# Stage 1 of a fused attention and gated-MLP kernel: one visit of the column halves for the early queries instead of two

## The chip, the cores and the metric

The kernel runs on one core of a Trainium2 chip. The metric is the device time of one execution in microseconds. The time before is 681.13 us, the median of three runs (680.72 to 682.45). The granted TensorE clock of the profiled execution is 0.999 of full speed over the whole span.

## The reference, cut to what matters

The program computes three stages one after another: plain attention with rotary positions, a gated MLP with spatial mixing, and a top-2 mixture of four causal attention experts. The change lies in the first stage alone:

```python
scores = scale * np.matmul(q_rot, k_rot.transpose(0, 1, 3, 2))   # 4 x 8 heads, 576 x 576, head_dim 64
scores = scores - np.max(scores, axis=-1, keepdims=True)
attn = np.exp(scores)
attn = attn / (np.sum(attn, axis=-1, keepdims=True) + 1e-09)
return np.matmul(attn, v)
```

## The kernel before, in words

Stage 1 works on 16 groups, each a pair of heads of one batch entry (`Work`, group number n). In a group the 576 queries of two heads make nine score blocks x = 0 to 8 of 128 rows: x = 2i + j is query block i of head j, and block 8 holds the last 64 queries of both heads. `slot(k)` (line 526) writes one step of the pipeline; k = 9n + x, and there are 9 slots in a group. The text calls them slot 0 to slot 8, and T5 is the start of the first score product that slot 5 issues. Lines 634 and 47 to 61 fix the order on TensorE (PE), ScalarE (ACT), VectorE (DVE) and GpSimd (POOL) to the order in which the code is written (`keep_in_program_order`). Most DMAs on SyncE's queue (SP) are not in that fixed order; the framework places them.

In slot x the code issues, in this order:

- on ACT the exponentials of block x (`exps`, line 449), which read the block's scores in PSUM (tile ps_S, two buffers) and write tile e (four buffers); in slots 0 and 4 also a copy of the finished products of the group before (`out`);
- on PE the scores of block x+1 (`scores`, line 434: four products of 288 columns, six for block 8), then the four transposes of block x-1 (`turn`, line 454, into ps_t, two buffers), then in slots 4, 5, 7, 0 and 1 one transpose of the 64 leftover keys (`turn_left`, into ps_l);
- on DVE the row maxima of block x+1 (`maxima`, tile nmax), and in odd slots a small gather of leftovers;
- the copy of the transposed block x-1 from PSUM to g0 or g1 (`place`, line 459): ACT for head 0 (even blocks), DVE for head 1 (odd blocks);
- on PE the products with the values (`av`, line 487). Queries 256 to 575 are done in slots 1 and 3 of the next group. Queries 0 to 255 of the group need the placed blocks 0 to 3 (g0) and are done in three parts: key blocks 0 and 1 in slot 5, key blocks 2 and 3 in slot 7, the leftover keys in slot 8. In the first two parts the weights are 64 columns wide: head 0 writes partitions 0 to 63 and head 1 partitions 64 to 127 of tile ps_o, so each head uses its own half of the array's columns (64-column records, `128*64` in the trace). The text calls such a run of 64-column products a visit. The leftover part is one product of full width;
- the preparation of the groups n+1 and n+2: rotary products on POOL (`rope`, slots 4 and 7), splits into high and low parts on DVE and POOL (`parts`, slots 1 and 3), whose DMAs fill the key operand kh (`fill_k`) that the scores of the next group's block 0 read in slot 8, and loads (slots 3 and 4).

After each slot the main loop (lines 648 to 666) advances side work: conversion of a weight for stage 2 (`convert_in`, some slots of all groups; its DVE steps use the same PSUM tile ps_l as `turn_left`), and from group 4 on, once per group, one step of `attended(bx, 0)` (line 268), which prepares stage 2's input: a load step (one DMA sa<-xr, three DMAs sr<-rd; groups 4, 6, 8, 13), a norm step (a POOL product and a DMA; groups 5, 7, 9, 14) or a part step (an ACT cast and a POOL subtraction; groups 10, 11, 12, 15).

Of the kernel before, what the change touches and what calls it, by code (L numbers as in the profile page):

```python
# [44 lines left out]
def fused_kernel(ctx, tc, qk, v, w_in, w_out, w_sg, g_ln, b_sg, wqk, wvg, wo, rope, cst, out):  # L45
# [222 lines left out]
    def attended(pool, b):  # L268


        ts = {}

        def load(c):
            ts[c] = a, r = [pool.tile([P, S], F32, tag="s" + x, name="s" + x, bufs=k) for x, k in (("a", 3), ("r", 2))]
            nc.sync.dma_start(a, xraw[b][c])
            factor_in(r, rd[b][c])

        def norm(c):
            a, r = ts[c]
            POOL.tensor_tensor(a, a, r, op=ALU.mult)  # L280
            nc.sync.dma_start(xd[b][c], a)

        def part(c):
            if c == 0 and b == 1:
                t = wc.tile([P, 2, 4, S], F32R, tag="w", name="x")
                xs[b] = [t[:, 0], t[:, 1]]
            elif c == 0:
                xs[b] = [pool.tile([P, 4, S], F32R, tag="x" + x, name="x" + x) for x in "hl"]
            split(*[x[:, c] for x in xs[b]], ts[c][0])

        order = (((load, 0), (norm, 0), (load, 1), (norm, 1), (load, 2), (norm, 2), (part, 0), (part, 1),
                  (part, 2), (load, 3), (norm, 3), (part, 3)) if b != 1 else
                 ((load, 0), (norm, 0), (load, 1), (norm, 1), (part, 0), (load, 2), (norm, 2), (part, 1),
                  (load, 3), (norm, 3), (part, 2), (part, 3)))
        for do, c in order:
            do(c)
            yield
# [3 lines left out]
    def leftover(pool, b):  # L301

        a, r = [pool.tile([P, S], F32, tag="s" + x, name="e" + x, bufs=k)[:, 0:512]
                .rearrange("p (c i n) -> p c i n", c=4, i=2) for x, k in (("a", 3), ("r", 2))]
        for i in range(2):
            nc.sync.dma_start(a[:, :, i, :], xraw[b + i][:, :, 512:S].rearrange("c p n -> p c n"))
            for j in range(2):
                h = slice(64 * j, 64 * j + 64)
                d = rd[b + i][:, 4, h].rearrange("(o c) n -> o c n", o=1)
                nc.sync.dma_start(r[h, :, i, :], d.to_broadcast([64, 4, 64]))  # L310
        yield
        POOL.tensor_tensor(a, a, r, op=ALU.mult)
        yield
        xe[b] = [pool.tile([P, 4, P], F32R, tag="e" + x, name="e" + x) for x in "hl"]
        split(*[x.rearrange("p c (i n) -> p c i n", i=2) for x in xe[b]], a)
        yield
# [7 lines left out]
    with ExitStack() as st:  # L324
# [7 lines left out]
        wk = st.enter_context(tc.tile_pool(name="a_wk", bufs=2))  # L332
# [193 lines left out]
        def slot(k):  # L526


            n, x = divmod(k, 9)
            (nk, xk), (nn, xn) = divmod(k - 1, 9), divmod(k + 1, 9)  # L530
            w, p, wk, wn, nx = [works.get(i) for i in (n, n - 1, nk, nn, n + 1)]

            if w:
                w.exps(x)
            if x == 0 and p:
                p.out(False)
            if x == 4 and p:
                p.out(True)

            if wn:  # L540
                if xn == 0:
                    wn.start()
                wn.scores(xn)
            if wk:
                wk.turn(xk)
            for at, g, i in ((4, w, 0), (5, w, 1), (7, w, 2), (0, p, 3), (1, p, 4)):
                if x == at and g:
                    g.turn_left(i)
            if x == 1 and p:
                p.turn_factor()  # L550

            if wn:
                wn.maxima(xn)
            for at, g, i in ((1, w, 0), (3, w, 1), (5, w, 2), (7, w, 3), (0, p, 4)):
                if x == at and g:
                    g.gather(i)
            if x == 0 and p:
                p.factor(0)

            if n == 0 and x in (2, 3):  # L560
                works[1].rope(3 - x, (2,), DVE)
            if wk:
                wk.place(xk)
            if x == 0 and p:
                p.factor(1)
            if x == 2 and p:
                p.place_left(True)
                p.store_factor()
            if x == 5 and w:
                w.place_left(False)  # L570

            if x in (1, 3) and p:
                p.av(True, x // 2)
            if x in (5, 7, 8) and w:
                w.av(False, {5: 0, 7: 1, 8: 2}[x])

            if nx:
                if x == (4 if n == 0 else 1):
                    nx.parts(0, DVE if n else ACT)
                if x == 3:  # L580
                    nx.parts(1, DVE if n else ACT)
                if n + 2 < B * NP:
                    if x == 3:
                        works[n + 2] = Work()
                        works[n + 2].load(n + 2)
                    if x == (7 if n == 0 else 4):
                        works[n + 2].rope(0)
                    if x == (8 if n == 0 else 7):
                        works[n + 2].rope(1)
                if x == 4 and n + 2 < B * NP:  # L590
                    works[n + 2].load_values()
# [37 lines left out]
        def warmed(n):  # L629

            for _ in range(n):
                PE.matmul(warm[:, 0:P], zero, zero, start=True, stop=True)
# [15 lines left out]
        for k in range(9 * B * NP + 7):  # L648
            n, x = divmod(k, 9)
            slot(k)  # L650
            if k < 4:
                warmed(2)
            if x in W_AT[4 if n == NP * B - 1 else min(n, 2 + n % 2)]:
                next(wload, None)
            if k == 9 * 4:
                steps = attended(bx, 0)
            if k == 9 * 14:
                lsteps = leftover(bx, 0)
            if n >= 4 and x == 8:
                next(steps, None)  # L660
            if n >= 14 and x == 3:
                next(lsteps, None)
            if k == 9 * 15 + 1:
                nsteps = attended(bx, 1)
            if k > 9 * 15 and x in (1, 5):
                next(nsteps, None)
# [37 lines left out]
    with ExitStack() as st:  # L704
        def pool(name, bufs):
            return st.enter_context(tc.tile_pool(name=name, bufs=bufs, reuse_waits="tile"))

        psum(st, t=1, c=1, S=3)
        wst, sm, ge, wp, wk, bg = (pool("b_st", 1), pool("b_sm", 2), pool("b_ge", 1), pool("b_w", 1),
                                   pool("b_wk", 2), pool("b_big", 1))  # L710
# [204 lines left out]
        for b in range(1, B):  # L915
# [7 lines left out]
            if b == 2:  # L923
                w = wc.tile([P, 12, DM], F32R, tag="w", name="w")
# [28 lines left out]
    with ExitStack() as st:  # L953
# [4 lines left out]
        sm, wk, bg, ptp = (pool("c_sm", 2), pool("c_wk", 2), pool("c_bg", 1), pool("c_pt", 1))  # L958
# [462 lines left out]
        w, g = works[2 * B - 1], op[B - 1]  # L1421
# [103 lines left out]
```

## Time and profile before

| what | value |
|---|---|
| median of three runs | 681.13 us |
| the profiled execution's own time | 678.8 us |
| its span, first to last instruction | 677.0 us |
| PE busy | 666.6 us (98%) |
| DVE, ACT, POOL busy | 454.1, 426.2, 342.6 us |
| granted TensorE clock | 0.999 |
| stage 1 | from about 13 to 271 us of the span |

Times are from one profiled execution. A row of the timeline gives the start of a run of like instructions in us from the start of the span, how long the run lasted to the end of its last instruction, the engine, the line (here that of a helper, so the tile names tell the instructions apart: ps_S are scores, ps_t and ps_l transposes, ps_o products with values, g placed blocks, e exponentials), the shape, the number of instructions, and in brackets the idle time before it with what ended it. PE's instructions are pipelined: the end of a run overlaps the start of the next, so the cost of a run is read from start to start. A float32 product makes two records. PEld is the weight load of TensorE.

### The profile page before, as it was taken

To read this page: it belongs to the slowest core of one execution; us is meant where nothing else is said; L and a number is where in the kernel's file an instruction comes from. 1 tells how busy PE (TensorE), PEld (TensorE's weight loads), DVE (VectorE), ACT (ScalarE), POOL (GpSimd) and SP (SyncE) were. 2 spreads that over 40 slices of the span, in tenths; PEclk is the share of its full clock that TensorE was granted. 3 is DMA by queue.
4 is the path that set the end of the run, shared out by engine and by line. 5 is a ranking of instruction groups with operands and counts; after the bars stand their busy time and mean duration, and the time that the engine had idled before them with its cause. 6 is when DMAs were issued, how large, how long until landed. Compare 5 with 4: busy or idle time off the path is not lost.

```text
span 677.0 us, 13577 instructions
## 1 busy us (share of the span) xinstructions
PE 666.6 (98%) x4741; PEld 585.9 (87%) x4741; DVE 454.1 (67%) x1026; ACT 426.2 (63%) x1018; POOL 342.6 (51%) x333
## 2 busy tenths in 40 slices
PE   8999999999999999999999999999999999999997
PEld 8777777777777777798999899899999999999985
DVE  5877777777787767478974764665247667666674
ACT  6777676777777777574472472472147776666774
POOL 2877777788888861462446217306313451542320
PEclk9999999999999999999999999999999999999999
DMA  7698887888788762652365234045556364453522
GB/s 271 197 282 246 258 235 210 247 243 248 229 250 249 215 175 80 190 157 80 118 186 176 88 108 135 16 132 161 128 167 163 76 185 93 131 158 81 142 82 78
DMA packets 64930, 112.84 MB, mean 167 GB/s; under 512 B 19471, under 2 KB 24670, under 8 KB 64862
## 3 DMA queue, kind: packets, MB, share of 16 engines
q1 hardware_dynamic: 62126, 106.30, 54.3%
q10 hardware_dynamic: 2736, 5.68, 2.8%
q8 instruction: 38, 0.62, 0.4%
q14 instruction: 30, 0.25, 0.1%
HBM read 58.06 MB, written 18.98 MB: 114 GB/s over the span
## 4 chain that ended last, share of the span: by engine, by line
PE 85%; DVE 5%; DMA 4%; ACT 2%; issue 1%; POOL 1%; SPq 1%; ACTq 0%; POOLq 0%; DVEq 0%
PE ps_S L59 45%; PE ps_o L59 16%; PE ps_t L59 13%; PE ps_f L59 5%; PE ps_l L59 3%; PE ps_s L59 3%; DVE nmax L59 1%; DMA ws<-in_w_sg_dram 1%; DVE ga L59 1%; DMA kh<-hi 1%; DMA mask<-in_cst_dram 1%; DVE g L59 1%; ACT ga L59 1%; DMA xr<-xt 1%; ACT e L59 1%
## 5 line engine op out<-in xcount | busy, mean ns | idle before, releaser
L59 ACT ACTIVATE e<-ps_S,nmax 128x576 f32<-128x576 f32 x144 | 108.0, 750 | 68.0 <-DVE nmax L59 67.8
L59 DVE TENSOR_REDUCE nmax<-ps_S 128x1 f32<-128x576 f32 x144 | 108.6, 755 | 57.3 <-PE ps_S L59 55.0
L59 PE MATMUL ps_t<-ident,e 128*128 128x128 f32 x776 | 120.6, 273 | 0.0
L59 PEld LDWEIGHTS ps_t<-ident,e 128*128 128x128 f32 x776 | 94.9, 140 | 3.8 <-ACT wih L59 0.4
L59 PE MATMUL ps_S<-kh,q 128*128 128x288 f32 x352 | 86.3, 337 | 2.6 <-ACT e L59 1.6
L59 POOL TENSOR_TENSOR t<-t,rp 128x576 f32<-128x576 f32 x60 | 84.4, 1429 | 0.1
L59 PEld LDWEIGHTS ps_S<-kh,q 128*128 128x128 f32 x352 | 53.2, 189 | 31.0 <-issue 10.7
L59 PE MATMUL ps_o<-g,v 128*64 128x320 f32 (+1 forms) x512 | 76.6, 418 | 0.4 <-DVE g L59 0.4
L59 POOL TENSOR_TENSOR lo<-t,hi 128x576 fp32r<-128x576 f32 x30 | 43.3, 1444 | 49.1 <-DVE hi L59 47.8
L59 PE MATMUL ps_S<-lo,qz 128*128 128x288 f32 x304 | 65.1, 296 | 0.0
L59 PEld LDWEIGHTS ps_o<-g,v 128*64 128x64 f32 x512 | 31.3, 136 | 25.1 <-issue 9.5
L59 PE MATMUL ps_S<-yh,w 128*128 128x288 f32 x256 | 51.8, 304 | 0.0
L59 POOL TENSOR_TENSOR yl<-x,yh 128x640 fp32r<-128x640 f32 (+1 forms) x16 | 25.1, 1569 | 51.1 <-ACT yh L59 50.9
L59 ACT ACTIVATE e<-e,nmax 128x128 f32<-128x128 f32 (+4 forms) x72 | 42.3, 588 | 13.6 <-DVE nmax L59 13.6
L59 PEld LDWEIGHTS ps_S<-lo,qz 128*128 128x128 f32 x304 | 48.5, 188 | 0.0
L59 ACT COPY g<-ps_t 128x512 f32<-128x512 f32 x80 | 46.8, 585 | 1.4 <-PE ps_t L59 0.8
L59 DVE COPY g<-ps_t 128x512 f32<-128x512 f32 x64 | 43.5, 680 | 1.3 <-PE ps_t L59 1.3
L59 POOL TENSOR_TENSOR t<-t 128x576 f32<-128x576 f32 x28 | 39.8, 1421 | 2.2
L59 PEld LDWEIGHTS ps_S<-yh,w 128*128 128x128 f32 x256 | 38.7, 189 | 0.1
L59 ACT ACTIVATE ga<-ga 128x512 f32<-128x512 f32 (+1 forms) x34 | 22.3, 656 | 25.8 <-DVE ga L59 25.8
L59 DVE CUSTOM_DVE_ANT_0 e<-ps_s,mask 128x128 f32<-128x128 f32 (+3 forms) x64 | 31.0, 485 | 8.1 <-PE ps_s L59 6.3
L59 PE MATMUL ps_S<-wsh,vh 128*128 128x288 f32 x160 | 34.6, 297 | 0.8 <-DVE u L59 0.5
(286 smaller groups left out, 1734.8 us busy)
## 6 DMA issues: line engine op xcount, KB each, us to landing
t<-in_qk_dram SPq DMA_DIRECT2D x32, 576.0 KB, 4.4
kh<-hi SPq DMA_DIRECT2D x92, 144.0 KB, 2.7
q<-hi SPq DMA_DIRECT2D x38, 144.0 KB, 2.4
qz<-hi SPq DMA_DIRECT2D x38, 144.0 KB, 3.1
q<-lo SPq DMA_DIRECT2D x38, 144.0 KB, 2.7
v<-in_v_dram SPq DMA_DIRECT2D x16, 320.0 KB, 3.0
sa<-xr SPq DMA_DIRECT2D x16, 288.0 KB, 3.6
xd<-sa SPq DMA_DIRECT2D x16, 288.0 KB, 2.9
```

The costliest lines, as they stand in the source:

```text
L59: ins = op(*a, **k)
```

## The change

Three edits, all in stage 1. In groups 0 to 14 (`nx` exists) slot 5 no longer turns and places block 4; slot 6 does so just before block 5, behind the scores of block 7. In the same groups the second part of the products for queries 0 to 255 (key blocks 2 and 3) moves from slot 7 to slot 5, right behind the first part. In groups 4 to 15 the step of `attended` runs after slot 4 instead of after slot 8. Group 15 keeps its old order of turns and products.

```diff
--- before.py
+++ after.py
@@ -541,7 +541,10 @@
                 if xn == 0:
                     wn.start()
                 wn.scores(xn)
-            if wk:
+            late = nx and x == 6
+            if wk and not (nx and x == 5):
+                if late:
+                    wk.turn(4)
                 wk.turn(xk)
             for at, g, i in ((4, w, 0), (5, w, 1), (7, w, 2), (0, p, 3), (1, p, 4)):
                 if x == at and g:
@@ -559,7 +562,9 @@
 
             if n == 0 and x in (2, 3):
                 works[1].rope(3 - x, (2,), DVE)
-            if wk:
+            if wk and not (nx and x == 5):
+                if late:
+                    wk.place(4)
                 wk.place(xk)
             if x == 0 and p:
                 p.factor(1)
@@ -571,8 +576,9 @@
 
             if x in (1, 3) and p:
                 p.av(True, x // 2)
-            if x in (5, 7, 8) and w:
-                w.av(False, {5: 0, 7: 1, 8: 2}[x])
+            if w:
+                for part in {5: (0, 1) if nx else (0,), 7: () if nx else (1,), 8: (2,)}.get(x, ()):
+                    w.av(False, part)
 
             if nx:
                 if x == (4 if n == 0 else 1):
@@ -656,7 +662,7 @@
                 steps = attended(bx, 0)
             if k == 9 * 14:
                 lsteps = leftover(bx, 0)
-            if n >= 4 and x == 8:
+            if n >= 4 and x == 4:
                 next(steps, None)
             if n >= 14 and x == 3:
                 next(lsteps, None)
```

## Rows read from the trace of the kernel before

**Rows 1.** The page, part 1: busy time of each engine.

```profile
PE 666.6 (98%) x4741; PEld 585.9 (87%) x4741; DVE 454.1 (67%) x1026; ACT 426.2 (63%) x1018; POOL 342.6 (51%) x333
```

**Rows 2.** Busy time by stretch, groups 3 to 10 whole; last columns clock, DMA share, GB/s.

```profile
62.84:190.03 127.19, 127.19 (x946) 98.55 (x945) 95.75 (x197) 93.07 (x241) 98.12 (x71) 1.00 0.83 239
```

**Rows 3.** Timeline of PE, group 8, slots 5 to 8 and the next slot 0.

```profile
151.14 0.51 PE L59 MATMUL ps_S<-kh,q 128*128 128x288 f32 x2
...
151.75 0.60 PE L59 MATMUL ps_t<-ident,e 128*128 128x128 f32 x4
152.19 0.27 PE L59 MATMUL ps_l<-ident,e 128*128 128x128 f32 x1
152.39 1.08 PE L59 MATMUL ps_o<-g,v 128*64 128x256 f32 x8
153.41 0.53 PE L59 MATMUL ps_S<-kh,q 128*128 128x288 f32 x2
...
154.04 0.60 PE L59 MATMUL ps_t<-ident,e 128*128 128x128 f32 x4
154.39 0.76 PE L59 MATMUL ps_S<-kh,q 128*128 128x288 f32 x4
...
155.70 0.27 PE L59 MATMUL ps_l<-ident,e 128*128 128x128 f32 x1
...
156.92 0.53 PE L59 MATMUL ps_S<-kh,q 128*128 128x288 f32 x2
...
158.23 0.61 PE L59 MATMUL ps_S<-kh,q 128*128 128x288 f32 x2
...
159.38 0.27 PE L59 MATMUL ps_l<-ident,e 128*128 128x128 f32 x1
159.43 0.40 PE L59 MATMUL ps_S<-kh,q 128*128 128x288 f32 x1
```

**Rows 4.** Timeline of the weight loads, group 8, at the end of slot 5's visit.

```profile
153.40 0.30 PEld L59 LDWEIGHTS ps_S<-kh,q 128*128 128x128 f32 x2 [0.39 <-ACT tl L59]
```

**Rows 5.** Timeline of DVE, group 8: the placing of block 3.

```profile
151.55 0.68 DVE L59 COPY g<-ps_t 128x512 f32<-128x512 f32 x1
```

**Rows 6.** Timeline of PE and DVE, group 0, slot 5: its visit and the placing before it.

```profile
22.95 0.65 PE L59 MATMUL ps_o<-g,v 128*64 128x256 f32 x2
23.28 0.67 DVE L59 COPY g<-ps_t 128x512 f32<-128x512 f32 x1
...
24.01 1.08 PE L59 MATMUL ps_o<-g,v 128*64 128x256 f32 x6 [0.41 <-DVE g L59]
```

**Rows 7.** Timeline of PE: a single visit in group 9, a double one in stage 1's tail.

```profile
160.81 1.30 PE L59 MATMUL ps_o<-g,v 128*64 128x320 f32 x8
...
273.52 2.37 PE L59 MATMUL ps_o<-g,v 128*64 128x320 f32 x16
```

**Rows 8.** Timeline of ACT, group 8: block 6 placed, exponentials of block 8.

```profile
155.90 0.59 ACT L59 COPY g<-ps_t 128x512 f32<-128x512 f32 x1
156.38 0.75 ACT L59 ACTIVATE e<-ps_S,nmax 128x576 f32<-128x576 f32 x1
157.02 0.20 ACT L59 ACTIVATION_READ_ACCUMULATOR e<-ps_S,nmax 128x1 f32 x1
```

**Rows 9.** Timeline of PE: groups 1, 2 and 12, the waits around slots 7 and 8.

```profile
42.76 0.60 PE L59 MATMUL ps_t<-ident,e 128*128 128x128 f32 x4
43.57 0.30 PE L59 MATMUL ps_l<-ident,e 128*128 128x128 f32 x1 [0.20 <-DVE wt L59]
...
61.55 0.49 PE L59 MATMUL ps_S<-kh,q 128*128 128x288 f32 x2 [0.79 <-DMA kh<-hi]
...
221.14 0.50 PE L59 MATMUL ps_S<-kh,q 128*128 128x288 f32 x2 [0.26 <-DMA xr<-xt]
```

**Rows 10.** DMA issues: the page (KB, us to landing), then SP's timeline in group 8.

```profile
kh<-hi SPq DMA_DIRECT2D x92, 144.0 KB, 2.7
...
151.10 2.86 SPq L154 DMA_DIRECT2D kh<-hi  x4
...
158.04 0.63 SPq L179 DMA_DIRECT2D sr<-rd  x1
```

## The prediction

> **What bounds the kernel now.** I read the page's busy times first: PE is busy for 98% of the span, every other engine for 67% or less [rows 1]. [...] So in stage 1 PE's own order of work sets the end, and the question is what PE's chain of starts becomes. For that I read PE's timeline of group 8 from start to start [rows 3]. What to see there: slot 5 starts at 151.14 and the next group's slot 1 at 159.43, 8.29 us later; all that the change moves on PE lies between. Last come the rows of DVE and ACT that would release PE if PE came earlier [rows 5, 8], for a PE that shows no idle time now may hide waits that it meets just in time.
>
> **What the change removes.** A visit of the column halves now takes 1.02 us, from 152.39 to 153.41 [rows 3]. Doubling it is cheaper than two: 16 records of 320 columns take 2.37 us where 8 take 1.30 [rows 7], 1.07 for eight more, which by columns is 0.86 for 256. A visit less its entry of 0.20 (152.19 to 152.39) gives 0.82; I take 0.84. What a second visit costs beyond its products is seen at its end: the next weight load stands still for 0.39 us [rows 4]. Without any new wait, slots 5 to 8 would be: slot 5, the leftover transpose at 0.61 (151.14 to 151.75, where block 4's turn stood), the visit at 0.81, then 1.02 + 0.84, so slot 6 at 2.67; slot 6, 0.98 (153.41 to 154.39) plus four transposes, 0.44 (151.75 to 152.19), 1.42; slot 7 without its visit, 1.31 to the leftover transpose (154.39 to 155.70) and 0.05 to the next scores (159.38 to 159.43), 1.36; slot 8 unchanged, 1.31 (156.92 to 158.23). Sum 6.76 against 7.09 now: 0.33 saved per group.
>
> **First new wait: DVE's placing of block 3.** Head 1's products read block 3, which DVE places from 151.55 to 152.23 [rows 5], 1.09 after the start of slot 5. Today the visit starts at 1.25, behind block 4's transposes, so the wait is hidden by 0.16. With these transposes gone PE is ready at 0.81. What happens then stands in group 0: head 0's two records start at 22.95, the rest waits for DVE until 24.01, although PE has nothing else to do; DVE's copy ended at 23.95, so the release takes 0.06 [rows 6]. In-order, head 0's lead is no use, as head 1's products still have to run whole. So head 1 starts at 1.15, not 0.81, and slot 6 starts at 1.15 + 1.02 + 0.84 = 3.01, slot 7 at 4.43. DVE cannot be earlier: this placing stands behind the maxima of block 5, which wait for slot 4's scores, and nothing there is moved. The wait, 0.34, eats the whole saving.
>
> **Second new wait: ACT in slot 8.** The scores that slot 0 issues go into the PSUM buffer that block 8's exponentials free. In group 8 ACT places block 6 at 155.90 (1.51 after slot 7 starts, just behind the transposes), starts the exponentials at 156.38 and ends their accumulator read at 157.22 [rows 8], 2.83 after slot 7's start, 2.89 with the release. Now the visit covers this: slot 0 starts 3.84 after slot 7 does. Without it PE comes at 1.36 + 1.31 = 2.67. So slot 0 starts at 4.43 + 2.89 = 7.32 instead of 7.10, and after a wait its scores take 0.63 (153.41 to 154.04), its transposes 0.44 and 0.05: the next slot 1 at 8.44 against 8.29 today. **Each regular group gets 0.15 us longer.**
>
> **What costs nothing.** ACT's placing of block 4 moves to slot 6. It starts 1.27 after that slot's start (0.63 + 0.44 + 0.20), frees ACT 0.48 later (155.90 to 156.38), so block 7's exponentials end near 2.6; the scores that need their buffer come at 1.42 + 1.36 = 2.78. If that cover is gone, PE waits up to 0.5 there. Block 4's tile e is held one slot longer, until slot 7's leftover transpose (1.31 + 0.27), before the exponentials of block 8 at 1.99 write over it. The step of `attended` at slot 4 instead of slot 8: four part steps put an ACT cast behind slot 4's copy, where ACT now has slot 5's placing time to spare, and a POOL subtraction ahead of the slot 7 rope products instead of behind them, so POOL ends the same; four norm steps move a POOL product and one DMA likewise; four load steps move four DMA issues on SP, about 0.6 each [rows 10], behind the kh issues of slot 3. Nobody needs these results before later groups. Bounds for the three together: 0.3 gained or lost in each of the twelve groups at worst, as no row shows POOL's or SP's order after the change; I take nothing, since all of them have more than a slot of room.
>
> **Groups that differ.** Group 0's visit waits already [rows 6], so it pays the 0.84 and 0.44 in full and gets back 5.04 - 4.01 = 1.03 from slot 7 on: +0.25. Group 1's leftover transpose in slot 7 waits for the weight conversion on DVE (43.57, where 42.76 + 0.44 = 43.20 would do [rows 9]); slot 7 comes over a microsecond later after slot 5 in the new order, so most of these 0.37 go: -0.2. In groups 2 and 12 slot 8 waits for a transfer, 0.79 and 0.26 of shown idle time [rows 9]; slot 8 would start at 5.79 against 5.78 now, so the transfer still ends last: 0. Group 15 keeps its order. Sum: 11 x 0.15 + 0.25 - 0.2 = +1.7; rounding in twelve terms can make 0.15 into 0.11 or 0.19, and I put the sum at 1.6. The profiled execution took 678.8 us with a span of 677.0; the median shown is 681.13, 2.3 higher, and the difference is applied to the median: 682.7.
>
> **Rivals.**
> (1) The waits do not bind, and the saved visit is a gain. With the first wait gone, the second would still hold slot 0 at 2.67 + 1.42 + 2.89 = 6.98, slot 1 at 8.10: 0.19 saved, over some 13 groups 2.5 us, 678.6. With both gone, 0.33 x 13 = 4.3, 676.8. For it speaks that PE has no idle time now [rows 2]; against it group 0, which waits in just this place [rows 6]. [...] Chance 0.17.
> (2) Transfers. The load steps' four issues (sa, three sr) come to stand ahead of kh's four in groups 4, 6, 8 and 13. The last kh issue of group 8 ends at 153.96 and lands some 2.7 later, 156.66, and the scores that read it start at 156.92 [rows 3, 10]: 0.26 of room. SP's order isn't fixed by the code, and it decides as soon as two of the four go first: 4 x 0.6 - 0.26 = 2.1 per group, 8 in all, 691; with one or two ahead 683 to 686. Against it: the code issues them a slot behind kh. Chance 0.10.
> (3) The order on PE, ACT, DVE and POOL is written out, so that the change does nothing is excluded, except for SP.
>
> **How the numbers follow.** A measurement of this kernel can tell 0.3%, 2.04 us, from no change. The forecast has 0.70 (0.03 is left for what I don't see); by its rounding and the bounds of the side steps about a quarter of it lies beyond +2.04, the rest within. Slower: 0.18 + 0.10 = 0.28. Faster: rival 1 nearly whole, 0.16. Same: 0.56. The range takes the forecast with its bounds (681 to 685) and reaches into rival 1's nearer case: 678.2 to 685.2. The likeliest case alone: 681.3 to 684.
>
> **What would show it.** In the changed trace, slot 5's ps_o run should split as in rows 6, with two records first and an idle weight load released by DVE g of some 0.3 us in groups 1 to 14; slot 6 should start 3.0 after slot 5; the first scores of slot 0 should carry a wait for ACT e, 2.9 after slot 7; a regular group should take 16.05 us instead of 15.90; the number of 64-column visits should fall by 15. No wait of the first kind, or a period below 15.8, proves rival 1. New waits for kh in groups 4, 6, 8, 13 prove rival 2. I am wrong in size if slot 6 starts later than 3.1, which would mean that the longer visit costs more than its products.

## The result, and the profile after

The changed kernel takes 685.79 us, the median of seven runs (682.97 to 688.89), the kernel before beside it 681.01 (679.66 to 682.45): 1.0072 times as long, 95% interval 1.0045 to 1.0099. Measured again later, beside the first try at t behind kh below, it was 681.94 against 679.37, 1.0038 [1.0017, 1.0058]. It is slower both times; the forecast was no change (682.7, range 678.2 to 685.2).

The profiled execution took 687.6 us with a span of 685.8, 8.8 longer than before's. All 8.8 lie in stage 1: from its end on, both kernels need 410 to 411 us. The page's busy times of the changed kernel:

```profile
PE 670.0 (98%) x4741; PEld 594.9 (87%) x4741; DVE 456.6 (67%) x1026; ACT 428.2 (62%) x1018; POOL 341.9 (50%) x333
```

Busy time by stretch, groups 3 to 10 whole (last columns clock, DMA share, GB/s), in this execution:

```profile
64.02:198.87 134.85, 130.09 (x947) 104.24 (x945) 97.25 (x198) 94.29 (x241) 97.33 (x71) 0.99 0.79 225
```

and the same eight groups in the profiled execution of its second measurement:

```profile
62.87:191.32 128.45, 128.19 (x945) 102.45 (x944) 96.87 (x198) 94.44 (x241) 98.75 (x72) 1.00 0.84 236
```

In [rows 2] PE was busy for all of 127.19. The second execution adds 1.26, or 0.16 a group, with one wait for a transfer (0.26, in group 8); its undisturbed groups take 16.02, 0.12 more than before's 15.90 (127.19 / 8), a price paid in every group. The first adds 6.4 more, and 4.76 of its stretch is PE idle: a price that differs from execution to execution. They have different causes.

**The price of every group.** PE's timeline of group 11, from slot 5 to the next slot 1 (the answer to [rows 3]):

```profile
191.56 0.51 PE L59 MATMUL ps_S<-kh,q 128*128 128x288 f32 x2
...
192.17 0.27 PE L59 MATMUL ps_l<-ident,e 128*128 128x128 f32 x1
192.37 2.27 PE L59 MATMUL ps_o<-g,v 128*64 128x256 f32 x16
...
195.99 0.77 PE L59 MATMUL ps_S<-kh,q 128*128 128x288 f32 x4
...
197.33 0.51 PE L59 MATMUL ps_S<-kh,q 128*128 128x288 f32 x2
...
198.87 0.53 PE L59 MATMUL ps_S<-kh,q 128*128 128x288 f32 x2
...
199.96 0.51 PE L59 MATMUL ps_S<-kh,q 128*128 128x288 f32 x2
```

DVE's placing of block 3 in the same group (answer to [rows 5]), the weight loads behind the visit and at the start of the next slot 0 (answer to [rows 4]), and ACT's exponentials of block 8 (answer to [rows 8]):

```profile
191.97 0.68 DVE L59 COPY g<-ps_t 128x512 f32<-128x512 f32 x1
```

```profile
194.57 0.30 PEld L59 LDWEIGHTS ps_S<-kh,q 128*128 128x128 f32 x2 [0.38 <-ACT e L59]
...
198.87 0.30 PEld L59 LDWEIGHTS ps_S<-kh,q 128*128 128x128 f32 x2 [0.30 <-ACT e L59]
```

```profile
197.98 0.74 ACT L59 ACTIVATE e<-ps_S,nmax 128x576 f32<-128x576 f32 x1
198.61 0.20 ACT L59 ACTIVATION_READ_ACCUMULATOR e<-ps_S,nmax 128x1 f32 x1
```

Slot 6 starts 3.01 after slot 5 (194.57 - 191.56; forecast 3.01), slot 7 at 4.43 (4.43), slot 0 at 7.31 (7.32), slot 1 at 8.40 (8.44, and 8.29 before). DVE ends the placing at 192.65, and in the trace the first record of head 1 starts at 192.70, as the first new wait had it. Slot 0 starts 0.06 behind ACT's accumulator read (198.81), as the second had it.

**The price that varies.** What PE waited for in stage 1 of the first execution (us in total, times, longest):

```profile
PE ps_S L59 <- DMA kh<-hi: 4.8, 3, 2.5
PE ps_S L59 <- ACT e L59: 2.9, 3, 1.3
```

Before, the first row was 0.8, once. Of the three waits in the second row two are in group 0, where the kernel before has them too; the third, 1.31, is at slot 8 of group 4. The longest wait for kh is in group 8. First PE's scores of slot 8, then the clock by stretch around them, then SP's issues ahead of them:

```profile
163.88 0.58 PE L59 MATMUL ps_S<-kh,q 128*128 128x288 f32 x2 [2.54 <-DMA kh<-hi]
```

```profile
160.50:163.80 3.30, 0.83 (x8) 0.59 (x6) 1.11 (x3) 1.73 (x5) 3.30 (x3) 1.00 0.69 170
163.80:167.40 3.60, 3.52 (x14) 3.35 (x15) 1.45 (x2) 1.31 (x4) 1.79 (x2) 0.55 0.74 256
167.40:170.40 3.00, 3.00 (x24) 2.17 (x22) 2.13 (x6) 2.28 (x6) 0.00 (x0) 0.97 0.65 219
```

```profile
156.59 0.36 SPq L365 DMA_DIRECT2D t<-in_qk_dram  x1
157.05 3.40 SPq L154 DMA_DIRECT2D kh<-hi  x4
160.55 1.82 SPq L511 DMA_DIRECT2D xr<-xt  x3
```

PE stood still for 2.54 us, and for the next 3.6 the granted clock was 0.55 of full speed: slot 8 took 2.20 and slot 0 1.87, where they take 1.30 and 1.10 after a short wait, 1.7 more. SP's rows show a load of raw queries or keys, t<-in_qk, ahead of the four kh transfers. SP's order belongs to the compiled kernel; both profiled executions of the changed kernel have the same. One t load stands ahead of kh in groups 2, 4 and 12 of the kernel before, and in groups 2, 4, 6, 8 and 12 of the changed one. The trace of before had its two transfer waits in groups 2 and 12 [rows 9].

Behind group 0 the first execution waited 1.31, 1.31, 0.91 and 2.54 us at slot 8 of groups 2, 4, 6 and 8, all with t ahead of kh, and nowhere else for more than 0.2. Its 8.8 us are, from these rows, some 1.5 for PE's order (13 groups of 0.12), 5.1 for groups 6 and 8 (3.45 of waits and 1.7 at the lower clock), where only the changed kernel has t ahead, and 1.8 more waiting in groups 2 and 4, where the kernel before has it too. But the order alone doesn't decide: the second execution, with the same order, waited only the 0.26.

So the theory to test was: (A) a t load ahead of kh delays kh; the moved step of `attended` adds such groups; PE's new order adds the small fixed price. Its rival (B): kh is late for another reason, and the order of t and kh doesn't matter.

### The profile page after: what moved, and what is told of

Read it like the earlier page. It is cut to its first block, busy times and chain, and to the rows that moved or that the text cites. A ratio compares the mean times of both kernels' runs of the same rounds, so it can differ in the third digit from the quotient of the medians.

```text
span 685.8 us, 13567 instructions
## 1 busy us (share of the span) xinstructions
PE 670.0 (98%) x4741; PEld 594.9 (87%) x4741; DVE 456.6 (67%) x1026; ACT 428.2 (62%) x1018; POOL 341.9 (50%) x333
## 4 chain that ended last, share of the span: by engine, by line
PE 82%; DVE 5%; DMA 5%; ACT 2%; issue 2%; SPq 1%; POOL 1%; ACTq 0%; DVEq 0%; POOLq 0%
PE ps_S L59 44%; PE ps_o L59 16%; PE ps_t L59 12%; PE ps_f L59 4%; PE ps_l L59 3%; PE ps_s L59 3%; DMA kh<-hi 2%; DVE nmax L59 1%; SPq L154 1%; DMA mask<-in_cst_dram 1%; DMA ws<-in_w_sg_dram 1%; DVE ga L59 1%; ACT e L59 1%; DMA sr<-rd 0%; DVE g L59 0%
## 5 line engine op out<-in xcount | busy, mean ns | idle before, releaser
L59 PE MATMUL ps_t<-ident,e 128*128 128x128 f32 x776 | 118.8, 274 | 0.2
L59 PEld LDWEIGHTS ps_o<-g,v 128*64 128x64 f32 x512 | 40.2, 136 | 22.6 <-issue 7.3
L59 POOL TENSOR_TENSOR xl<-sa,xh 128x576 fp32r<-128x576 f32 x12 | 17.7, 1480 | 42.0 <-ACT xh L59 35.9
```

The lines of the kernel that those rows point to most:

```text
L59: ins = op(*a, **k)
```

## The experiments

**One edit at a time.** Beside the same kernel before (680.3, median of 29 runs) ran the changed kernel with the step back at slot 8, and the kernel before with the step at slot 4.

In the changed kernel:

```diff
-            if n >= 4 and x == 4:
+            if n >= 4 and x == 8:
```

In the kernel before:

```diff
-            if n >= 4 and x == 8:
+            if n >= 4 and x == 4:
```

> The two edits on TensorE alone; the step of attended goes back behind slot 8. Theory T (the transfers): the step at slot 4 lets the framework put the load t<-in_qk of SP's queue ahead of the four kh<-hi in groups 6 and 8, and PE waits for kh there; the edits on PE cost only the two waits, 0.14 a group. Then this kernel takes 682.0 to 683.0, a regular group 16.0 to 16.1, and no wait for kh in groups 4, 6 and 8 above 0.3. Rival P (the new order on PE by itself makes kh late): 684.5 to 686, waits for kh over 0.8 in groups 4, 6 and 8.

> The kernel before with the step of attended behind slot 4, nothing else. Theory T: waits for kh of 0.5 to 2.5 in groups 4, 6 or 8, which the kernel before does not have; 683 to 685. Rival P: 680.5 to 681.7, no new wait for kh.

PE's edits alone: 682.55 (679.56 to 685.29), 1.0020 [1.0001, 1.0039]; regular groups 16.02, and one wait for kh, 0.31, in group 2. That is as theory T had it. The step alone: 682.34 (679.53 to 686.59), 1.0024 [0.9998, 1.0050]; this lies between the two theories, and the interval reaches no change. Regular groups take 15.90 as before, but in its profiled execution, the slowest of twelve, slot 7 of groups 2, 6, 8 and 12 took 4.95, 2.92, 4.29 and 4.96 instead of 2.53. The rows name kh in groups 2 and 12 (2.35 and 2.33), another transfer in group 8 (1.70) and ACT in group 6 (0.33).

SP's order has t ahead of kh in groups 2 and 4 with PE's edits alone, and in groups 2, 4, 6, 8 and 12 with the step alone. So the moved step adds groups 6 and 8; the two longest waits here are in groups where the kernel before has t ahead too, and group 2 is done before the first moved step runs. Each half costs about 2 us by medians. But single times spread by 6 us, so the shares were still uncertain.

**The merged visit without moving block 4's transposes.** The kernel before with one edit; the step stays at slot 8.

```diff
-            if x in (5, 7, 8) and w:
-                w.av(False, {5: 0, 7: 1, 8: 2}[x])
+            if w:
+                for part in {5: (0, 1) if nx else (0,), 7: () if nx else (1,), 8: (2,)}.get(x, ()):
+                    w.av(False, part)
```

> Only the merging of the visit in slot 5; block 4 is turned in slot 5 before it, as in the kernel before, and the step stays behind slot 8. Theory of the two waits: head 1's products find block 3 placed, so the first wait is gone; the wait for ACT's exponentials of block 8 stays. Slot 5 3.10, slot 6 0.98, slots 7 and 8 together 2.9, a group 15.70, so 0.2 less than before; 678.0 to 679.0. Rival: slot 8 comes 0.35 earlier against the transfers of kh, which then bind in most groups; 680 to 682. Rival: the first wait was not DVE's placing but the longer visit itself; then slot 5 is 3.4 and the kernel 682.5 or more.

679.71 (677.17 to 682.45), 0.9987 [0.9965, 1.0009]. Regular groups take 15.78 us, 0.12 less than before (15.70 was expected, and 678.0 to 679.0 in all), where the changed kernel's take 0.12 more. So merging is a gain in every regular group, though the total isn't clear of noise; moving block 4's transposes out from in front of the visit turns it into a loss.

**All loads of a group held in the written order.**

```diff
-                    if n < 2:
-                        tc.keep_in_program_order(d)
+                    tc.keep_in_program_order(d)
```

(and the same for the kh transfers)

> The changed kernel with the four kh<-hi and the loads t<-in_qk of stage 1 held in program order on SP, so that kh goes first in every group. Theory T: the waits for kh in groups 2 to 8 go, 681.5 to 683.0. Rival P: 684.5 to 686, as the waits stay. A third possibility: SP stands behind kh's wait for its cast and t comes late for rope on GpSimd, 684 and more with waits for t.

740.8 us, 1.0879: here t is issued a group later than otherwise, the rotary products on POOL wait for it (5.1, 6.2 and 5.2 us in groups 3, 4 and 5), what stands behind them comes late, and groups take 16.4 to 23.3 us. It says nothing on A and B, only that t must be early too.

**A first try at t behind kh.** The t loads are issued a group earlier in the code, in slot 5, and held behind kh; three kernels, and the changed kernel again.

```diff
+                ahead_ = 2 if n == 0 and x == 3 else 3 if x == 5 else 0
+                if ahead_ and n + ahead_ < B * NP:
+                    works[n + ahead_] = Work()
+                    works[n + ahead_].load(n + ahead_)
                 if n + 2 < B * NP:
-                    if x == 3:
-                        works[n + 2] = Work()
-                        works[n + 2].load(n + 2)
```

> The changed kernel once more, on the same chip as the three below. From the two halves measured apart (1.0020 for the edits on TensorE, 1.0024 for the step): about 1.0045 times the kernel before if the two add up, 1.007 as in the first measurement if the step costs more on top of the edits on TensorE.

> The kernel before with the same change of the load; kh goes first in every group. Theory T: the waits of groups 2 and 12 (0.86 and 0.33 in the first profile) go, 0.997 to 0.999. Rival: no difference, as these waits come from something else.

> The changed kernel, with the load t<-in_qk issued in slot 5 for three groups ahead (where the framework hoists it to anyway) and kh and t held in program order: t now goes behind kh on SP in groups 2, 6, 8 and 12, only group 4 still has it ahead. Theory T: waits for kh stay in group 4 alone, 1.0015 to 1.003 times the kernel before, what the edits on TensorE cost alone, or less. Rival (the DMA engines are simply too full, whoever goes first): 1.004 or more, with waits for kh or t elsewhere.

> The merged visit behind block 4's transposes, with the load behind kh in every group. Theory T: 15.78 for every group from 2 to 14, 0.995 to 0.997 times the kernel before, the fastest of all. Rival: slot 8 now comes 0.1 to 0.2 earlier against kh and waits appear, 0.998 or more.

Beside a kernel before of 679.37: change again 681.94; before with t behind kh 683.62, 1.0044 [1.0027, 1.0060]; changed kernel so 687.78, 1.0097; merged visit alone so 682.50, 1.0035. All were slower, by my own edit: it also put the loads of group 2 behind kh in group 0, whose rotary products came late (group 0 waited for q, up to 4.4 us). In the changed kernel so edited PE also waited for kh, 0.94, 2.00 and 1.89 in groups 2, 3 and 4, though t stands ahead of it in group 4 alone: the rival's sign, and a first hint that t ahead of kh isn't the only way to a late kh. The useful part is that in the kernel before so edited groups 2 to 10 took 15.89 to 15.96 and the waits of groups 2 and 12 were gone.

**The same without that flaw.** Group 0 issues its loads in slots 2 and 8, which leaves its order as it was.

```diff
-                ahead_ = 2 if n == 0 and x == 3 else 3 if x == 5 else 0
+                ahead_ = 2 if n == 0 and x == 2 else 3 if x == (8 if n == 0 else 5) else 0
```

The decisive pair is this order in the kernel before, against the same with one of the two t loads written in slot 3 ahead of kh in groups 1 to 12.

> The kernel before, with the loads of raw queries and keys (t<-in_qk) held behind the four kh transfers on SP in every group; group 0 keeps the order of before, which the earlier attempt did not. Theory A (a t load ahead of kh on SP delays kh and makes slot 8's scores wait): no PE wait for kh in any group, groups 2 to 14 at 15.90 us, the waits of groups 2 and 12 gone (0.86 and 0.33 in the trace of before), so 1 us less: ratio 0.998 to 1.000. Theory B (kh is late for other reasons, the order of t and kh does not matter): waits for kh remain in some groups, ratio 1.000 within 0.002.

> The same kernel as the one with t behind kh, with one difference: in groups 1 to 12 one of the two t loads (64 x 1152 elements twice, 576 KB) stands ahead of kh on SP. Theory A: waits of PE for kh at slot 8's scores in most of these twelve groups, 0.3 to 2 us each (2.4 in the worst groups seen so far), and where one is over 2 us a fall of the granted clock behind it: 5 to 15 us slower, ratio 1.007 to 1.022. Theory B: the same time as with t behind kh, within 0.2%, and no more waits than before has.

With t behind: 678.42 (677.81 to 680.73), 0.9972 [0.9956, 0.9988]. With t ahead: 685.69 (682.90 to 688.92), 1.0073 [1.0049, 1.0096]. The order of one load and kh is worth 7.3 us in twelve groups; A holds, B falls. A had waits in most of the twelve groups; the profiled execution with t ahead, the slowest of its eight, has them in six. PE's waits behind group 0, with t ahead (with t behind no row names kh):

```profile
PE ps_S L59 <- DMA kh<-hi: 7.2, 6, 2.2
```

SP's timeline in group 3, t ahead of kh, then PE's at the scores of slot 8 that read kh:

```profile
73.17 0.36 SPq L368 DMA_DIRECT2D t<-in_qk_dram  x1
73.63 2.41 SPq L154 DMA_DIRECT2D kh<-hi  x4
```

```profile
79.16 0.50 PE L59 MATMUL ps_S<-kh,q 128*128 128x288 f32 x2 [1.85 <-DMA kh<-hi]
```

The same two with t behind kh:

```profile
73.25 2.38 SPq L154 DMA_DIRECT2D kh<-hi  x4
...
78.23 0.91 SPq L367 DMA_DIRECT2D t<-in_qk_dram  x2
```

```profile
77.04 0.53 PE L59 MATMUL ps_S<-kh,q 128*128 128x288 f32 x2
```

The page's row of DMA issues (KB each, median us from issue to landing), with t behind, then with t ahead:

```profile
kh<-hi SPq DMA_DIRECT2D x92, 144.0 KB, 2.6
```

```profile
kh<-hi SPq DMA_DIRECT2D x92, 144.0 KB, 3.9
```

SP issues kh only 0.4 later (73.63 against 73.25), and with t behind, PE needs kh 1.41 after the last issue (75.63 to 77.04). With t ahead PE goes on 3.12 after it (76.04 to 79.16). So most of the delay isn't SP's time but the transfer's: kh's transfers of 144 KB each take 3.9 us to landing with t's 576 KB ahead of them and 2.6 with t behind. By what mechanism t holds kh up isn't shown, and whether t on another queue would spare kh wasn't tried.

**What is left in the changed kernel.** It and the merged visit with the same order of loads:

> The changed kernel with t behind kh on SP (all groups but group 4, where one t stays ahead). Theory A: no waits for kh except perhaps in group 4, regular groups 16.02 us, so what is left of the loss is the 0.12 to 0.15 per group of PE's own order: 1.5 to 2 us against before, ratio 1.002 to 1.003. Theory B: waits for kh in groups 2 to 8 as in the changed kernel, ratio 1.004 to 1.007.

> Only the merged visit (behind block 4's transposes, which stay where they were; the step of attended stays at slot 8), with t behind kh on SP. Theory A: regular groups 15.78 us as in the run of the merged visit alone, no waits for kh: 1.5 us less for the visit and 1 us less for the transfers, 676 to 678, ratio 0.995 to 0.998. Theory B: as the merged visit alone, 0.9987 within 0.002.

The merged visit: 677.42 (676.70 to 678.39), 0.9955 [0.9937, 0.9973], the best kernel of the study, ahead of both, though its profiled execution still has one wait for kh, 0.94 in group 3, where A had none. The changed kernel: 683.59 (679.47 to 688.29), 1.0039 [1.0014, 1.0064], more than A's 1.002 to 1.003 and widely spread, so t ahead of kh isn't all that its transfers suffer from. Its profiled execution, the shortest (679.47), shows what else there is. What SP's queue waited for in groups 4 to 9:

```profile
SPq L171 <- DMA t<-in_qk_dram: 6.3, 3, 2.8
```

L171 issues q: SP stood still until a t load had landed, and kh stands behind q. In that stretch the same kernel with the step at slot 8 and PE's old order has 1.9, twice. The longest of the three is in group 8:

```profile
146.54 0.73 SPq L171 DMA_DIRECT2D q<-hi  x1
150.16 0.46 SPq L171 DMA_DIRECT2D q<-lo  x1
```

POOL made the low part of this q from 145.32 to 146.74, so the rotary products didn't hold this q; SP's wait for t did, and t is a load for a later group. What the step changes in SP's order is that in groups 5, 7 and 9 its xd stands just ahead of t, and in groups 5 and 7 its three sr stand between t and q; with the step at slot 8 xd stands behind q, and the sr between t and q in groups 6 and 8. That t lands late because of this is argued from the order and not shown. Two kernels part PE's order from the step, both with t behind kh; a third takes away the first new wait by DVE's order alone.

```diff
+            early = wk and x == 4 and nx
+            if early:
+                wk.place(3)
             if wn:
                 wn.maxima(xn)
-            if wk and not (nx and x == 5):
+            if wk and not early and not (nx and x == 5):
```

> The changed kernel's work on PE (merged visit, block 4's transposes behind the next scores), but the step of attended back at slot 8, and t behind kh on SP in every group. Theory A (with the transfers out of the way only PE's own order is left, and that costs 0.12 per group): groups 2 to 14 at 16.02 us, no waits for kh, 1.3 to 1.8 us above the kernel before with the same order of loads (678.42 in the last comparison), so 679.7 to 680.3, single times within some 3 us of each other, ratio to before 0.998 to 1.001. Rival (PE's new order itself makes transfers late, whoever issues them): median 682 to 684, single times spread over 6 us or more, as with the step at slot 4.

> The kernel before with the step of attended at slot 4 and t behind kh on SP (all groups but group 4); PE's order as in before. Theory A (the step at slot 4 puts sr, xd and sa ahead of the t load and of q on SP, so t and with it q and kh come late even where t is behind kh): regular groups 15.90 where undisturbed, but median 1.5 to 5 us above the 678.42 of the same kernel with the step at slot 8, 680 to 683, and single times spread over 5 us or more. Rival (what was left in the changed kernel with t behind kh came from PE's new order): 678 to 679, spread under 3 us.

> As the run with PE's new order, the step at slot 8 and t behind kh, with one edit: in slot 4 DVE places block 3 ahead of the maxima of block 5. First wait as the prediction has it (the visit waits for DVE's placing of block 3, 0.34): placing ends 0.75 after the start of slot 5, the visit needs no wait, slot 5 takes 2.67 to 2.75 instead of 3.02, and the group 15.70 to 15.85 instead of 16.02, 3 to 4 us less in all. Rival (slot 5 is long because the merged visit costs more than its products): slot 5 stays above 2.9 and the group at 16.0. A third outcome: slot 5 gets short and the late maxima of block 5 make a new wait for ACT in slots 5 to 8, the group stays at 15.9 to 16.0.

In the two rows with the step at slot 4 one t stays ahead in group 4. The kernel before as it was took 680.31 beside rows 1, 4 and 6, and 680.46 beside the others.

| with t behind kh | median (range) | regular group |
|---|---|---|
| kernel before | 678.42 (677.81 to 680.73) | 15.90 |
| step at slot 4 | 680.45 (677.99 to 685.84) | 15.90 |
| PE's new order | 680.38 (679.79 to 686.84) | 16.02 |
| both, the changed kernel | 683.59 (679.47 to 688.29) | 16.02 |
| PE's new order, block 3 placed early | 678.67 (677.26 to 680.22) | 15.79 |
| merged visit alone | 677.42 (676.70 to 678.39) | 15.8 (15.73 to 15.93) |

By medians PE's order costs 1.96, seen in nearly every execution (9 of 13 between 679.79 and 681.79). One went to 686.84, past the spread that was expected. It is the profiled one, and its longest wait is for kh in group 3, though t stands behind:

```profile
80.24 0.82 PE L59 MATMUL ps_S<-kh,q 128*128 128x288 f32 x2 [2.69 <-DMA kh<-hi]
```

```profile
77.06 2.39 SPq L154 DMA_DIRECT2D kh<-hi  x4
```

Here kh was issued late, at 77.06 where the kernel before with t behind has 73.25. Ahead of that SP's queue had waited 2.2 us for a t load before it issued q, and 1.6 for a weight load (raw) before kh. So t ahead of kh is one way to a late kh, and not the only one.

The step costs 2.03 by medians, but its interval against the kernel before, [0.9975, 1.0029], overlaps that of t behind kh alone, [0.9956, 0.9988], and its times spread from 677.99 to 685.84. Its profiled execution (680.83) has no wait for a transfer: its span is 2.6 longer than that of the kernel before with t behind, 0.4 of it ahead of stage 1's last scores (266.24 against 265.88), the rest behind, with no cause shown. Together the two prices would make 682.4; measured 683.6. In the last two rows the visit is merged and PE's wait for block 3 is gone, but for 0.1 in the first of them. DVE's early placing and slot 5's visit of the changed order, then the visit of the merged visit alone:

```profile
150.30 0.69 DVE L59 COPY g<-ps_t 128x512 f32<-128x512 f32 x1 [0.71 <-PE ps_t L59]
```

```profile
150.13 0.51 PE L59 MATMUL ps_S<-kh,q 128*128 128x288 f32 x2
...
150.95 2.04 PE L59 MATMUL ps_o<-g,v 128*64 128x256 f32 x16
152.92 0.53 PE L59 MATMUL ps_S<-kh,q 128*128 128x288 f32 x2
```

```profile
150.71 0.51 PE L59 MATMUL ps_S<-kh,q 128*128 128x288 f32 x2
...
151.32 0.60 PE L59 MATMUL ps_t<-ident,e 128*128 128x128 f32 x4
151.76 0.27 PE L59 MATMUL ps_l<-ident,e 128*128 128x128 f32 x1
151.96 1.95 PE L59 MATMUL ps_o<-g,v 128*64 128x256 f32 x16
153.84 0.53 PE L59 MATMUL ps_S<-kh,q 128*128 128x288 f32 x2
```

From the visit's start to the next scores: 2.20 in the changed kernel (192.37 to 194.57), 1.97 with block 3 placed early, 1.88 behind block 4's transposes. DVE now ends at 150.99, 0.04 behind the start of the visit; with the release of 0.06 [rows 6], head 1 starts an estimated 0.10 behind head 0. So the first new wait is shown: 0.23 of slot 5 goes with DVE's order alone, and a group falls from 16.02 to 15.79. The total fell by 1.7, less than the 3 to 4 expected.

## Why the prediction was wrong, point by point

- **The removed visit, right.** A merged visit takes 1.88 to the next scores, forecast 1.02 + 0.84 = 1.86. Slots 5 to 8 of the changed kernel came within 0.04 of the forecast starts. The merged visit alone, with one visit less, takes 0.12 a group less (15.78 against 15.90).
- **First new wait, right in place and size, and its sign in the trace wrong.** The visit wasn't split into two records and a gap. Head 0's first two records run alone, head 1's first starts 1.14 after slot 5 (forecast 1.15), 0.33 behind head 0's, and from there the two heads alternate every 0.11 us instead of starting in pairs every 0.22. By that rhythm (the rows don't name the head) head 0's last record starts at 2.37, head 1's at 2.70. Placing block 3 early leaves some 0.10 of the 0.33 and gives back 0.23; the merged visit alone has no lag, and its visit is 0.32 shorter (1.88 against 2.20), close to the 0.34 forecast.
- **Second new wait, right**: 7.31 against 7.32. With the first wait gone it still holds slot 0, in the merged run 7.00 after slot 5 (157.71 - 150.71); rival 1 had 6.98.
- **The sum for PE's order, right in size**: 1.6 forecast, 1.96 measured by medians where t is behind kh, and 1.4 between the spans of the kernel before (677.0) and the changed one's second profiled execution (678.4). A regular group pays 0.12, not 0.15.
- **What costs nothing: here it failed.** The step of `attended` at slot 4 was costed at 0 with the reason that nobody needs its results before later groups. Its results were not the point; its place in SP's order was. With it moved, t stands ahead of kh in groups 6 and 8 too, and there the first execution lost 5.1 us. By medians the step costs 2.0 us by itself in the framework's order (682.34 - 680.3), and 2.0 where t is behind kh; neither is clear of noise alone, and what carries the second isn't shown. The bounds of 0.3 in each of twelve groups would have held 2.0, not the 5.1; the value taken was their middle, and SP's new order wasn't bounded by what a late kh costs PE.
- **Groups 2 and 12** were costed at 0 because the transfer still ends last. Their waits came from a t load ahead of kh: with t behind, they are gone in the kernel before, and it gains 0.28% [0.12, 0.44]. In the changed kernel's first execution group 2 waited 1.31 instead of 0.79, group 12 not at all.
- **Rival 2 (chance 0.10)** came nearest. It had the step, SP, the loads of groups 4, 6 and 8, and waits for kh, and with one or two issues ahead 683 to 686: the first measurement is 685.79. But it named sa and sr as what stands ahead, and priced it by issue time, 0.6 each. In the profiled execution t stood ahead, and what it costs is landing time, 1.3 us more for kh in the pair above. Its room of 0.26 counts kh's 2.7 from the end of the last issue, where the page's figure runs from the issue itself. It was also not counted that the clock can fall behind such a wait (1.7 us more in group 8), nor that the loss varies by execution.
- **Rival 1** didn't happen in the changed kernel, but is what the merged visit alone and block 3 placed early are, with 0.12 and 0.11 a group less where it had 0.19.

How much of the changed kernel's varying price comes from t ahead of kh and how much from a late q wasn't parted further; after t behind kh, 683.59 against 681.94 and 685.79 doesn't settle it. Why one execution falls into such waits and the next doesn't stays open.

## What to carry to other kernels

Before an idle-looking instruction is taken out from in front of a product, ask which wait it fills: block 4's transposes cost PE little in slot 5, since DVE was placing block 3 beside them and PE would have waited for that, and moving them turned a gain of 0.12 us a group into a loss of 0.12. Don't take a step that issues DMAs as free to move where the framework orders the queue: compare the queue's order before and after, and price a small transfer that someone waits for by what now stands ahead of it, not by issue time alone: here kh took 1.3 us longer to land behind one 576 KB load (3.9 against 2.6). Where the single times of a kernel spread by 1% and another order of loads makes them steady, the spread itself is the finding.

## What the runs showed of the hardware

- kh's 144 KB transfers took 3.9 us to land (the page's median) where one 576 KB load was issued just ahead of them on the same queue in groups 1 to 12, and 2.6 where it was issued behind them; in group 3 their issue began only 0.4 us later (73.63 against 73.25).
- The granted clock fell to half of full speed behind some waits of PE: it was 0.55 for 3.6 us behind the 2.54 in group 8 of the changed kernel, and 0.50 from 81 to 83 behind the 2.69 in group 3 with PE's new order and t behind kh. With t ahead of kh in the kernel before, a wait of 2.24 in group 10 was followed by 0.50, the second row here; behind the wait of 1.85 in group 3 it stayed at 1.00, the first. The expectation's line at 2 us isn't shown, the length of the wait alone doesn't tell: the execution with the step alone has waits of 2.35 and 2.33, and a mean clock of 0.998 over its 684.8 us, as the changed kernel's over 685.8 with its one fall. By an estimate from these figures that has room for one such fall, not for two.

```profile
79.16:81.50 2.34, 2.34 (x18) 2.29 (x19) 1.50 (x3) 0.75 (x3) 1.42 (x1) 1.00 0.93 288
...
197.60:199.60 2.00, 2.00 (x9) 1.89 (x8) 1.12 (x3) 1.21 (x4) 2.00 (x2) 0.50 1.02 361
```

- The two heads' 64-column products run side by side: in group 8 of the kernel before, where both are ready, their records start within 0.01 us of each other, and the last three pairs follow at 0.22 us. Where head 1 starts 0.33 late, in group 11 of the changed kernel, they alternate every 0.11 and the visit is longer by 0.32 than the merged visit alone (2.20 against 1.88); where DVE's placing ends 0.04 behind the start of the visit, by 0.09 (1.97).
